# A linear-attention and SwiGLU kernel: PSUM as one rotating pool of single banks, half-height loads in natural head order, stores of 64 partitions, and a reordered start

## The chip, the cores and the metric

The kernel runs on one core of one Trainium2 chip. The time is the device time of one execution in microseconds (us), and I quote the median of several runs. The profile is of one execution; its "span" goes from the first to the last instruction and is about 2 us shorter than the time.

Names of the engines: PE is TensorE (matmuls), PEld its weight loads, DVE is VectorE, ACT is ScalarE, POOL is GpSimd, SP issues transfers. A name with a small q (SPq) is the engine's instruction queue. SBUF and PSUM are the two memories in which the kernel keeps its tiles: tiles of up to 128 partitions in SBUF, which its loads fill, and the tiles in PSUM that its matmuls write.

## The reference

There are 8 batches of 8 heads with 576 positions and head dimension 64; `d_model` is 512, `d_ff` is 1536, and there are 4608 tokens. In float32:

```python
q_s = softmax of q over the head dimension
k_s = softmax of k over the 576 positions
kv  = einsum('bhsd,bhse->bhde', k_s, v)
att = einsum('bhsd,bhde->bhse', q_s, kv)
x   = att.transpose(0, 2, 1, 3).reshape(4608, 512)
out = (silu(x @ w_gate) * (x @ w_val)) @ w_out
```

The two gate and value products and the output product are nearly all of the arithmetic.

## The kernel before

A batch's heads are handled in two groups of four. A group's life is: load q, k, v; exponentials on ACT (`eq`, `ek`) and a cast of v (`vb`); the norm on DVE (`rs`, `rr`, `qs`); nine transposes on PE (`tp`) copied to `qt`; the product `kv`; its scaled block-diagonal copy `bd`; the product `xp`, copied to `xt`. Then come the gate and value matmuls over chunks of tokens (`g_ps`, `u_ps`, the result `hr`) and the output tiles (`o_ps`, copied to `o_sb`, stored). The lines show the parts that changed; cuts are marked.

```python
aps = pool("aps", bufs=1, PSUM)      # one buffer of TWO banks: tp, kv, xp take turns
fps = pool("fps", bufs=6, PSUM)      # six single banks: g_ps, u_ps, o_ps, x_tail
...
def load(b, G, what, src):           # one transfer over all 128 partitions, 576 KB
    t_ = ld.tile([128, 2, T * 64], FP32, tag=what, name=what)
    ap = AP(offset=src[b, 4 * G], ap=[[T * 64, 128], [2 * HSTR, 2], [1, T * 64]])
    dmas[what, b, G] = nc.sync.dma_start(out=t_, in_=ap)
...
def att_exp(b, G):                   # eq and ek on ScalarE, then
    nc.gpsimd.tensor_copy(out=vb[...], in_=raw["v", b, G])
    ...                              # and the norm: rs, rr, qs on VectorE
...
def store(j, o_sb):                  # 128 tokens in one transfer, where both halves are of one batch
    parts = [(0, 128, [[d_model, 2], [T * d_model, 64], [1, d_model]], b0, t0)]
    ...
        nc.sync.dma_start(out=dst, in_=o_sb[p0:p1, :])
...
    for G in range(NG):              # batch 0, before any gate/value matmul
        att_t(0, G); att_kv(0, G); att_x(0, G)
    ...
    for m in range(MT):
        m_unit(0, 576, m)
    o_pair(0); o_pair(2)             # four output tiles, and after them all of batch 1
    for G in range(NG):
        att_exp(1, G)
    for G in range(NG):
        att_t(1, G); att_kv(1, G); att_x(1, G)
    ...
    for ci, (c0, n) in enumerate(chunks):          # (576, 448), then chunks of 512
        ...
        for m in range(MT):                        # 12 units
            if m in (4, 8):
                if att:
                    att_exp(b, ...); steps = att_steps(b, ...)
                if ci > 0:
                    o_pair(...)
            m_unit(c0, n, m)
            if m % 4 > 0 and m > 4 and steps:
                steps.pop(0)()
```

The weights are cut into slices of columns, each loaded by four transfers whose row order fits the head order of the 128-partition loads.

The softmax here doesn't subtract the row's maximum and nothing guards it: scores larger than these inputs give would overflow.

## Time and profile before

The kernel took 381.04 us (median of 3; 379.97 to 381.15). The span of the profiled run is 378.1 us. Four boundaries, all read from the timeline of PE, cut it into stages:

| stage | from | to | us |
|---|---|---|---|
| start and batch 0's gate/value work | 0 | first output tile, 48.93 | 48.9 |
| four output tiles and batch 1's attention | 48.93 | first gate matmul of chunk 576, 77.42 | 28.5 |
| chunk 576..1023 | 77.42 | first gate matmul of the next chunk, 110.75 | 33.3 |
| the other chunks | 110.75 | PE's end, 360.93 | 250.2 |
| tail | 360.93 | 378.1 | 17.2 |

These are lines of the page of the kernel before. The rows of digits show tenths of busy time (or of the granted PE clock) in 40 slices of the span, 9.5 us each. The last line is the chain of waits, by engine.

```profile
span 378.1 us, 4831 instructions
...
PE 320.0 (85%) x1857; PEld 161.1 (43%) x1888; DVE 171.8 (45%) x304; ACT 152.7 (40%) x196; POOL 41.5 (11%) x57
...
PE   0379994487689999999999999999999999999910
...
PEclk9999998578989999999999999999999999999975
DMA  8799951885230606430661246110010011012011
...
PE 77%; DVE 6%; DMA 6%; ACT 4%; issue 2%; SPq 0%; DVEq 0%
```

PE is the bound where its digit is 9. That leaves the first three slices, slices 7 to 12 (57 to 113 us, with the clock low in five of the six), and the last two, in which PE has hardly any work. From slice 13 to there, PE's own work sets the pace. The next view lists the waits of PE (us in total, times, longest).

```profile
PE tp L145 <- DVE qs L132: 19.9, 4, 9.0
PE kv L161 <- DVE qt L149: 9.2, 4, 4.6
PE g_ps L205 <- ACT xt L191: 4.1, 7, 0.6
PE tp L145 <- ACT xt L191: 2.1, 2, 1.0
```

The last line is the price of the single two-bank buffer: the second group's transposes wait until the first group's `xp` is copied away. The timeline shows what happens in the batch 1 stage (start, length, engine, line, operation, and in brackets the idle time before it and its releaser):

```profile
60.58 0.69 DVE L238 COPY o_sb<-o_ps 128x512 f32<-128x512 f32 x1 [2.99 <-DMA out_dram<-o_sb]
...
64.28 1.14 PE L145 MATMUL tp<-ident,qs 128*128 128x128 bf16 x9 [4.83 <-DVE qs L132]
...
68.06 1.16 PE L161 MATMUL kv<-vb_79,ek 64*128 64x129 bf16 x18 [2.63 <-DVE qt L149]
...
72.29 1.12 PE L145 MATMUL tp<-ident,qs 128*128 128x128 bf16 x9 [1.05 <-ACT xt L191]
```

The chain runs through a store: the output copy waits 2.99 us for a buffer that a store still reads, the norm is queued behind that copy on DVE, and PE waits 4.83 us for the norm. Last, three windows of 2 us. The columns are: start and end, length, busy time and count of PE, PEld, DVE, ACT, POOL, then the granted PE clock, the DMA share (mean busy share of the core's 16 DMA engines) and GB/s.

```profile
4.00:6.00 2.00, 0.00 (x0) 0.00 (x0) 0.10 (x1) 1.16 (x1) 0.00 (x0) 1.00 1.05 395
6.00:8.00 2.00, 0.00 (x0) 0.00 (x0) 1.93 (x3) 1.16 (x1) 0.00 (x0) 1.00 1.01 392
92.00:94.00 2.00, 2.00 (x7) 0.76 (x6) 0.94 (x3) 0.39 (x1) 0.00 (x0) 0.50 0.91 308
366.00:368.00 2.00, 0.00 (x0) 0.00 (x0) 0.00 (x0) 0.00 (x0) 0.00 (x0) 0.50 0.13 51
```

At 92 to 94 us the clock is at half. At 366 us only the last stores run, with a share of 0.13 and 51 GB/s: as much as two of 16 engines.

### The profile page before, as it was taken

Reading aid. Unit: us, or ns where it says so; the run is one execution under the profiler, and the core shown is the slowest. Engines: PE = TensorE matmul, PEld = TensorE weight load, DVE = VectorE, ACT = ScalarE, POOL = GpSimd, SP = SyncE. Lnnn points to the kernel's source line nnn. Section 1 sums busy time; section 2 is a strip of 40 time slices with the busy share of each in tenths; the row PEclk is TensorE's granted clock in tenths of the full one; section 3 lists DMA queues with packets and bytes.
Section 4 is the critical chain, followed back from the end, with each engine's and each line's share of the span. In section 5 each row is a group of like instructions: output and inputs, shape, how many; then the busy total and the mean of one; then the engine's idle time right before and its main releaser. Section 6 shows DMA issues by size and latency. Waiting matters only on the chain.

```text
span 378.1 us, 4831 instructions
## 1 busy us (share of the span) xinstructions
PE 320.0 (85%) x1857; PEld 161.1 (43%) x1888; DVE 171.8 (45%) x304; ACT 152.7 (40%) x196; POOL 41.5 (11%) x57
## 2 busy tenths in 40 slices
PE   0379994487689999999999999999999999999910
PEld 0157752333344444444444444444444444444400
DVE  3523436335544664547364727555664333333200
ACT  3333360147736273645466454736273113121000
POOL 2995020011110101010101100110000000000000
PEclk9999998578989999999999999999999999999975
DMA  8799951885230606430661246110010011012011
GB/s 297 135 154 179 289 209 51 284 311 178 83 135 19 211 18 212 142 118 29 217 207 52 56 186 208 40 40 17 31 54 27 10 47 44 13 44 67 18 51 44
DMA packets 24071, 42.78 MB, mean 113 GB/s; under 512 B 1520, under 2 KB 7152, under 8 KB 24048
## 3 DMA queue, kind: packets, MB, share of 16 engines
q1 hardware_dynamic: 17856, 37.75, 28.8%
q0 software_dynamic: 6192, 4.72, 8.9%
q8 instruction: 15, 0.25, 0.3%
q14 instruction: 8, 0.07, 0.1%
HBM read 37.75 MB, written 9.44 MB: 125 GB/s over the span
## 4 chain that ended last, share of the span: by engine, by line
PE 77%; DVE 6%; DMA 6%; ACT 4%; issue 2%; SPq 0%; DVEq 0%
PE u_ps L205 24%; PE g_ps L205 24%; PE o_ps L233 20%; DMA out_dram<-o_sb 4%; PE kv L161 3%; ACT xt L191 3%; PE tp L145 3%; PE xp L183 2%; DMA q<-in_q_dram 2%; DVE qs L132 2%; DVE rs L128 2%; ACT eq L114 1%; DVE qt L149 1%; DVE o_sb L238 1%; ACT L114 1%
## 5 line engine op out<-in xcount | busy, mean ns | idle before, releaser
L213 ACT ACTIVATE sg<-g_ps 128x512 bf16<-128x512 f32 (+2 forms) x120 | 65.0, 554 | 148.9 <-PE g_ps L205 134.6
L214 DVE TENSOR_TENSOR hr<-sg,u_ps 128x512 bf16<-128x512 bf16 (+2 forms) x120 | 74.9, 633 | 108.1 <-PE u_ps L205 106.2
L205 PE MATMUL g_ps<-xt,wg 128*128 128x512 bf16 (+2 forms) x468 | 114.1, 366 | 4.5 <-ACT xt L191 4.1
L205 PE MATMUL u_ps<-xt,wv 128*128 128x512 bf16 (+2 forms) x475 | 112.3, 363 | 0.3
L233 PE MATMUL o_ps<-wo,hr 128*128 128x512 bf16 x422 | 95.3, 379 | 0.5
L205 PEld LDWEIGHTS <-wv 128*128 128x128 bf16 x480 | 47.7, 99 | 48.2 <-issue 2.7
L205 PEld LDWEIGHTS <-wg 128*128 128x128 bf16 x480 | 45.7, 100 | 48.9 <-issue 8.7
L233 PEld LDWEIGHTS <-hr 128*128 128x128 bf16 x432 | 42.0, 98 | 50.2
L238 DVE COPY o_sb<-o_ps 128x512 f32<-128x512 f32 x36 | 23.9, 686 | 32.0 <-PE o_ps L233 26.2
L128 DVE TENSOR_REDUCE rs<-eq 128x18 f32<-128x1152 bf16 x16 | 21.6, 1352 | 33.8 <-ACT eq L114 33.8
L191 ACT CAST xt<-xp 128x1024 bf16<-128x1024 f32 x16 | 16.2, 1012 | 41.8 <-PE x_tail L186 41.8
L145 PE MATMUL tp<-ident,qs 128*128 128x128 bf16 x144 | 12.8, 245 | 22.2 <-DVE qs L132 19.9
L122 POOL CAST vb_79<-v 128x1152 bf16<-128x1152 f32 x8 | 9.8, 1221 | 138.6 <-PE kv L161 90.7
L145 PEld LDWEIGHTS <-qs 128*128 128x128 bf16 x144 | 10.8, 110 | 26.4 <-DVE qs L132 21.2
L132 DVE TENSOR_TENSOR qs<-eq,rr 128x1152 bf16<-128x1152 bf16 x16 | 21.7, 1358 | 0.5
L114 ACT ACTIVATE eq<-q 128x1152 bf16<-128x1152 f32 x16 | 18.6, 1162 | 5.1 <-DMA q<-in_q_dram 5.0
L118 ACT ACTIVATE ek<-k 128x1152 bf16<-128x1152 f32 x16 | 18.4, 1149 | 0.6 <-DMA k<-in_k_dram 0.6
L114 ACT ACT_TABLE_LOAD x14 | 18.0, 1283 | 1.0 <-PEq L322 0.7
L213 ACT ACT_TABLE_LOAD x14 | 18.0, 1283 | 0.2
L122 POOL CAST vb_80<-v 128x1152 bf16<-128x1152 f32 x8 | 9.8, 1223 | 70.2 <-PE kv L161 62.7
L161 PEld LDWEIGHTS <-ek 64*128 64x128 bf16 x288 | 10.2, 107 | 15.8 <-issue 9.1
L149 DVE COPY qt<-tp 128x640 bf16<-128x640 bf16 (+1 forms) x32 | 13.1, 450 | 3.7 <-PE tp L145 3.7
(28 smaller groups left out, 81.5 us busy)
## 6 DMA issues: line engine op xcount, KB each, us to landing
q<-in_q_dram SPq DMA_DIRECT2D x16, 576.0 KB
k<-in_k_dram SPq DMA_DIRECT2D x16, 576.0 KB
v<-in_v_dram SPq DMA_DIRECT2D x16, 576.0 KB
out_dram<-o_sb SPq DMA_DIRECT2D x32, 256.0 KB
wo<-in_moe_w_out_dram POOLq DMA_DIRECT2D x3, 512.0 KB, 9.7
out_dram<-o_sb SPq DMA_DIRECT2D x8, 128.0 KB
wg<-in_moe_w_gate_dram POOLq DMA_DIRECT2D x8, 96.0 KB, 3.3
wv<-in_moe_w_val_dram POOLq DMA_DIRECT2D x8, 96.0 KB, 3.8
```

Of the source, the lines that this page charges most:

```text
L114: nc.scalar.activation(out=eq, in_=raw["q", b, G].rearrange("p h (t d) -> p t h d", d=64), func=AF.Exp)
L122: nc.gpsimd.tensor_copy(out=vb[:, :, 0:128].rearrange("p t (h d) -> p t h d", d=64), in_=raw["v", b, G].rearrange("p h (t d) -> p t h d", ...
L128: nc.vector.reduce_sum(out=rs, in_=eq2, axis=mybir.AxisListType.X)
L132: nc.vector.tensor_mul(qs.rearrange("p t (h d) -> p (t h) d", d=64), eq2, rr.to_broadcast([128, 2 * T, 64]),)
L145: nc.tensor.transpose(out=tp[:, bank, j * 128:(j + 1) * 128], in_=s["qs"][:, t, :], identity=ident)
L161: nc.tensor.matmul(out=kv[:, g, 0:129], lhsT=s["ek"][r, t, :, :].rearrange("p h d -> p (h d)"), rhs=s["vb"][r, t, 0:129], start=(t == 0), ...
L191: nc.scalar.copy(out=xt[:, 2 * G:2 * G + 2, c0:c0 + 512], in_=xp)
L205: nc.tensor.matmul(out=p_[:, 0:w_], lhsT=w[:, kk, ms], rhs=xt[:, kk, c:c + w_], start=(kk == 0), stop=(kk == KT - 1),)
L213: nc.scalar.activation(out=sg[:, 0:w_], in_=g_ps[:, 0:w_], func=AF.Silu)
L214: nc.vector.tensor_mul(hr[:, m, r:r + w_], sg[:, 0:w_], u_ps[:, 0:w_])
L233: nc.tensor.matmul(out=o_ps, lhsT=hr[:, m, r0:r0 + 128], rhs=wo[:, m, :], start=(m == 0), stop=(m == MT - 1),)
L238: nc.vector.tensor_copy(out=o_sb, in_=o_ps)
```

## The change

The intent: every PSUM tile becomes a single bank out of one rotating pool of eight, so that no group waits for another's banks. The q, k and v loads take the heads in their natural order, two transfers of 64 partitions each, so that a weight slice needs one transfer instead of four. A store always has 64 partitions as its first dimension. Batch 0's v is cast on ACT instead of POOL, and its two groups are interleaved. Batch 1's attention is woven between the output tiles. The `xp` eviction is split over two engines, and the last output tile is cut into two halves of columns. The core of the diff, with cuts marked:

```diff
-    aps = pool("aps", bufs=1, PSUM); fps = pool("fps", bufs=6, PSUM)
+    psp = pool("psp", bufs=8, PSUM)
...
     def load(b, G, what, src, second=None, after=None):
-            ap=[[T * 64, 128], [2 * HSTR, 2], [1, T * 64]],
-        dmas[what, b, G] = nc.sync.dma_start(out=t_, in_=ap)
+        for g in range(2):
+            ap = AP(offset=src[b, 4 * G + 2 * g], ap=[[T * 64, 64], [HSTR, 2], [1, T * 64]])
+            d = eng.dma_start(out=t_[64 * g:64 * g + 64], in_=ap)
...
     def w_slice(dst, src, c0, n):
-        for h in range(2):
-            for g in range(2): ...                 # four transfers of 64 rows
+        return nc.gpsimd.dma_start(out=dst[:, :, c0:c0 + n], in_=ap)
...
-        nc.scalar.copy(out=xt[:, 2 * G:2 * G + 2, c0:c0 + 512], in_=xp)
+        nc.scalar.copy(out=xt[:, 2 * G, c0:c0 + 512], in_=xp[0])
+        nc.vector.tensor_copy(out=xt[:, 2 * G + 1, c0:c0 + 512], in_=xp[1])
...
-            parts = [(0, 128, [[d_model, 2], [T * d_model, 64], [1, d_model]], b0, t0)]
+        for half in range(2):
+                ap=[[T * d_model, 64], [1, c1 - c0]],
+            engs[half].dma_start(out=dst, in_=o_sb[64 * half:64 * half + 64, c0:c1])
...
+        att_exp(0, 0, nc.scalar); att_exp(0, 1, nc.scalar)
+        att_norm(0, 0, BANKS); att_t(0, 0, nc.vector); att_kv(0, 0)
+        att_norm(0, 1, BANKS); att_t(0, 1, nc.scalar); att_kv(0, 1)
+        att_bd(0, 0); att_x(0, 0); att_bd(0, 1); att_x(0, 1)
...
-        o_pair(0); o_pair(2)                       # then batch 1's attention
+        att_head(1, 0); o_unit(0); att_head(1, 1)
+        o_unit(1); s0[0](); s0[1](); o_unit(2); s0[2](); s1[0](); s1[1]()
+        o_unit(3); s1[2]()
```

## The prediction

This was written before the changed kernel was built or run.

> **What bounds the kernel now.** TensorE: the page has it busy 320.0 of 378.1 us; the chain of waits is 77% PE. From 110.7 to 360.9 us it is bound for good: PE idles only about 0.64 us per chunk with an attention batch (waits by engine: for the ScalarE copy of xt, 1.01 us). So the gain must come from the ends and the first 110 us. By the timeline and the windows:
> - Start: gate/value matmuls run steadily only from 25.3 us. Both groups of batch 0 go through one PSUM buffer in turn.
> - Batch 1: its output tiles end at 59.5 us, the next chunk starts at 77.4. In between PE has some 6 us of work, and the granted clock falls to 0.50. The chain shows DVE rs and qs behind an o_sb copy that waited 2.99 us for a store, then tp, kv, xp serially.
> - Chunk 576..1023: PE waits 2.4 and 3.6 us for qs, and the clock falls after each.
> - Tail: PE ends at 360.9, the span at 378.1. With only stores running, the windows show DMA share 0.13 and 51 GB/s: 2 of 16 engines. [...] the store's destination starts with a dimension of 2. [...]
>
> **What the change does, in us**
> 1. Stores of 64 partitions[...]. Tail from PE's end: 17.2 now; then half-width copy (est. 0.4), issue 0.5, landing about 2: est. 3.5. Gain 13.5. The o_sb waits go too.
> 2. Start reordered: v cast on ScalarE (1.15), group 1's exp and norm under group 0, no single PSUM buffer. The new limit is v of group 1: it landed by 13.1, and now shares the DMA with weights that start about 1 us earlier; est. 15. Then cast, kv 1.2, bd 1.1, xp 1.2, eviction 0.6: steady at about 20. Gain 5.3. Weights then arrive just in time (est. 2.7 us per slice from 9.3); one DMA for four cuts Pool's issue from 2.4 to about 0.8 per slice.
> 3. Batch 1 woven between output tiles: DVE's order (norm, o_sb, norm, o_sb, qt, bd) makes xp of group 0 wait, about 2.4 us of PE idle. From the end of batch 0's gate/value work to the next chunk: 28.5 now, est. 17.6. Gain 10.9, plus 2.8 at the next chunk's start (no cold clock, no 1.2 us xt wait).
> 4. Chunk 576..1023: head and steps stand at the same units, so both qs waits stay. Gain 0.
> 5. Five later attention chunks: xt eviction split over two engines, 0.64 to about 0.2 each. Gain 2.2.
> 6. Natural head order, doubled loads (0.45 us issue each, off the chain), four small bd multiplies for two: about -0.3.
>
> Sum about 34.5: 381.0 to **346 us**, 8 in 10 between 339 and 354. Chances: faster 0.97, same 0.02, slower 0.01.
>
> **What would show it.** DMA share during stores well above 0.13, a tail under 5 us; steady gate/value work from 19 to 21 us; the chunk at 576 starting near 61 us; two qs waits of 2 to 4 us left in it; 34.8 us per attention chunk.
>
> **What would make it wrong.** Weights or batch 1's v arriving late (gate/value work stalled on DMA between 20 and 44 us); a clock drop in the batch 1 stage (+1.6); the shared pool's rotation making gate/value banks wait for kv or xp releases in every chunk (+5 or more).

13.5 + 5.3 + 10.9 + 2.8 + 0 + 2.2 - 0.3 is 34.4, written there as about 34.5. Before the run it was shown only that the old stores have a share of 0.13; that stores of 64 partitions would have a much larger one was the author's estimate. The runs showed it afterwards: 0.64 in the kernel after, 1.03 in the first store experiment.

The single figures of the steps, in brackets, against the traces of before and after: the half-width copy took 0.42 us (0.4), the issue of a store 0.51 to 0.85 before and 0.47 to 1.05 after (0.5), the last two stores, of 64 KB, landed 1.9 and 2.2 us after their issue (2), and the cast of v on ACT took 1.15 (1.15). In the old start `kv` took 1.16 us (1.2), the wait for `bd` 0.89 (1.1) and `xp` with its tail 1.14 (1.2); the eviction by halves took 0.59 on ACT (0.6). POOL issued the four weight transfers of a slice in 2.37 to 2.58 us before, and one in 0.75 to 0.88 after (2.4 and 0.8). For the 2.7 us per slice: after, the eight slices took 2.9 us each, from the first issue at 11.66 to the last landing at 35.0, with the loads and the transfers of `wo` beside them. The issue of a load took 0.41 to 0.47 us before and 0.60 to 0.61 after (medians; 0.45). "No cold clock" means a granted clock of 0.50 from 66 to 81 us before; after, it was at 1.00 from 66 to 80. The 1.6 us for a clock drop were an estimate; about 1.7 for each fall is what chunk 576 shows below.

## The result, and the profile after

| | median us | runs | ratio to before, 95% interval |
|---|---|---|---|
| before | 380.76 | 4 (379.97 to 381.15) | |
| after | 351.32 | 4 (350.33 to 352.68) | 0.9232 (0.9195 to 0.9268) |

All ratios in this document are the mean time of one kernel's runs over the mean time of the other's runs of the same rounds, so they are not quite the ratio of the quoted medians. Executions over 1.5% slower than the fastest of the same kernel are left out of the means. The kernel became 29.4 us faster, where 34.5 us was predicted. The same boundaries in both timelines say where the gain came from:

| stage | before | after | gain | predicted gain |
|---|---|---|---|---|
| start and batch 0's gate/value work, to | 48.93 | 50.06 | -1.1 | 5.3 |
| output tiles and batch 1, to | 77.42 | 67.98 | 10.6 | 10.9 |
| chunk 576..1023, to | 110.75 | 95.94 | 5.4 | 2.8 (all of it at the chunk's start) |
| other chunks, to | 360.93 | 344.10 | 2.0 | 2.2 |
| tail, to | 378.1 | 348.6 | 12.7 | 13.5 |
| added small costs | | | | -0.3 |
| sum | | | 29.5 | 34.4 |

The lines of the page after that answer to those shown of before:

```profile
span 348.6 us, 5035 instructions
...
PE 317.0 (91%) x1900; PEld 159.5 (46%) x1900; DVE 188.5 (54%) x354; ACT 152.6 (44%) x217; POOL 27.2 (8%) x31
...
PE   0269998998699999999999999999999999999994
...
PEclk9999999899999999999999999999999999999999
DMA  7999998999602990299029902990202021102123
```

The slices here are 8.7 us. The hole in slices 7 to 12 is mostly closed (what is left of it, digits of 8, 8 and 6, holds the waits shown below), the idle slices at the end are gone, and the clock dips in one slice. By the chain of waits PE's share rose from 77% to 80%. The first three slices are no better. The DMA row is fuller (slices of 9 where there were 4 and 6), though the bytes are the same (42.81 MB, and 42.78 before); that is the first sign of the miss. The waits of PE after:

```profile
PE tp L152 <- DVE qs L138: 19.4, 4, 9.9
PE xp L192 <- DVE bd_78 L184: 2.0, 2, 1.6
...
PE g_ps L213 <- DVE xt L201: 0.9, 5, 0.2
```

The waits of `kv` for `qt` (9.2 us) and of `tp` for `xt` (2.1 us) have left the list, and the steady wait for `xt` went from 4.1 us to 0.9. New, and left out here, are two waits of `kv` for `vb` at the start (1.6 and 1.3 us). The waits for `bd` are about as large as before (3.6 us over both groups then and now). Windows of the kernel after:

```profile
4.00:6.00 2.00, 0.00 (x0) 0.00 (x0) 0.00 (x0) 0.00 (x0) 0.00 (x0) 1.00 1.06 222
6.00:8.00 2.00, 0.00 (x0) 0.00 (x0) 0.70 (x1) 1.16 (x1) 0.00 (x0) 1.00 1.04 219
92.00:94.00 2.00, 2.00 (x27) 1.09 (x25) 1.44 (x4) 0.54 (x1) 0.00 (x0) 1.00 0.12 27
344.00:346.00 2.00, 0.11 (x1) 0.00 (x0) 0.42 (x1) 0.00 (x0) 0.00 (x0) 1.00 0.64 158
```

Here is the miss. In the same windows, with only the same loads running, the rate is 219 to 222 GB/s instead of 392 to 395, while the share is still about 1.05: all 16 engines are busy, and together they get just over half as much done (219 over 392 is 0.56). That is another picture than the old tail, where the share itself was 0.13. The third line has the clock at 1.00 where it was 0.50, which will matter below. The last line shows the new stores at a share of 0.64. The timeline shows the consequences at the start, and what stayed in the middle:

```profile
11.66 0.88 POOL L94 DMA_DIRECT2D wg<-in_moe_w_gate_dram  x1 [10.36 <-DMA v<-in_v_dram]
...
19.15 1.15 ACT L106 CAST vb_77<-v 128x1152 bf16<-128x1152 f32 x1 [1.38 <-DMA v<-in_v_dram]
...
61.06 0.39 PE L192 MATMUL xp<-qt,bd_78 128*128 128x512 bf16 x1 [1.57 <-DVE bd_78 L184]
...
80.12 0.68 PE L152 MATMUL tp<-ident,qs 128*128 128x128 bf16 x9 [2.41 <-DVE qs L138]
...
91.18 0.68 PE L152 MATMUL tp<-ident,qs 128*128 128x128 bf16 x9 [3.10 <-DVE qs L138]
```

The lines of the kernel before that answer to the cast of `vb_77` and to the two waits for `qs`:

```profile
13.10 1.75 POOL L122 CAST vb_80<-v 128x1152 bf16<-128x1152 f32 x1 [0.69 <-DMA v<-in_v_dram]
...
91.14 0.95 PE L145 MATMUL tp<-ident,qs 128*128 128x128 bf16 x9 [2.41 <-DVE qs L132]
...
104.37 0.68 PE L145 MATMUL tp<-ident,qs 128*128 128x128 bf16 x9 [3.61 <-DVE qs L132]
```

The second group's v reaches its cast at 19.15 us; in the kernel before, with its loads at 392 to 407 GB/s, the same cast started at 13.10. The first weight transfer starts only at 11.66, so weights cannot be what slows the loads at 4 to 8 us. In the middle the wait of `xp` for `bd` and the two waits for `qs` are there, as predicted. After the first of them the clock was at 0.50 from 62 to 64 us; after the two for `qs` it stayed at 1.00.

### The profile page after: what moved, and what is told of

It reads as the page before. It is cut to its first block, busy times and chain, and to the rows that moved or that the text cites. A ratio compares the mean times of both kernels' runs of the same rounds, so it can differ in the third digit from the quotient of the medians.

```text
span 348.6 us, 5035 instructions
## 1 busy us (share of the span) xinstructions
PE 317.0 (91%) x1900; PEld 159.5 (46%) x1900; DVE 188.5 (54%) x354; ACT 152.6 (44%) x217; POOL 27.2 (8%) x31
## 2 busy tenths in 40 slices
DMA packets 25577, 42.81 MB, mean 123 GB/s; under 512 B 2896, under 2 KB 8784, under 8 KB 25552
## 4 chain that ended last, share of the span: by engine, by line
PE 80%; DVE 7%; DMA 7%; ACT 3%; issue 1%; SPq 1%; DVEq 0%; ACTq 0%
PE u_ps L213 25%; PE g_ps L213 25%; PE o_ps L238 24%; DMA v<-in_v_dram 5%; PE kv L168 2%; PE tp L152 2%; DMA k<-in_k_dram 2%; DVE xt L201 1%; DVE hr L222 1%; PE xp L192 1%; DVE qs L138 1%; DVE rs L132 1%; ACT L118 1%; ACT eq L118 1%; SPq L76 1%
## 5 line engine op out<-in xcount | busy, mean ns | idle before, releaser
L238 PE MATMUL o_ps<-wo,hr 128*128 128x512 bf16 x420 | 94.1, 380 | 0.0
L238 PEld LDWEIGHTS <-hr 128*128 128x128 bf16 x420 | 40.7, 98 | 49.0 <-issue 0.8
L243 DVE COPY o_sb<-o_ps 128x512 f32<-128x512 f32 x35 | 23.2, 685 | 22.1 <-PE o_ps L238 22.1
L152 PE MATMUL tp<-ident,qs 128*128 128x128 bf16 x144 | 12.2, 236 | 19.5 <-DVE qs L138 19.4
L138 DVE TENSOR_TENSOR qs<-eq,rr 128x1152 bf16<-128x1152 bf16 (+2 forms) x18 | 21.9, 1224 | 0.5
L108 POOL CAST vb_76<-v 128x1152 bf16<-128x1152 f32 x7 | 9.2, 1310 | 150.3 <-DMA v<-in_v_dram 89.1
L152 PEld LDWEIGHTS <-qs 128*128 128x128 bf16 x144 | 9.9, 105 | 24.0 <-DVE qs L138 21.2
L200 ACT CAST xt<-xp 128x512 bf16<-128x512 f32 x16 | 9.4, 586 | 17.6 <-PE xp L192 9.4
L201 DVE CAST xt<-xp 128x512 bf16<-128x512 f32 x16 | 10.9, 684 | 3.4 <-PE x_tail L195 3.4
L108 POOL CAST vb_77<-v 128x1152 bf16<-128x1152 f32 x7 | 9.0, 1289 | 44.9 <-DMA v<-in_v_dram 24.9
## 6 DMA issues: line engine op xcount, KB each, us to landing
wv<-in_moe_w_val_dram POOLq DMA_DIRECT2D x2, 384.0 KB, 12.2
```

Of the source, the lines that this page charges most:

```text
L108: eng.tensor_copy(out=out, in_=in_)
L138: nc.vector.tensor_mul(qs[:, t0:t1, :].rearrange("p t (h d) -> p (t h) d", d=64), eq2[:, 2 * t0:2 * t1, :], rr[:, 2 * t0:2 * t1].to_broadc ...
L152: nc.tensor.transpose(out=tp[:, j * 128:(j + 1) * 128], in_=s["qs"][:, t, :], identity=ident)
L201: nc.vector.tensor_copy(out=xt[:, 2 * G + 1, c0:c0 + 512], in_=xp[1])
L238: nc.tensor.matmul(out=o_ps, lhsT=hr[:, m, r0:r0 + 128], rhs=wo[:, m, :], start=(m == 0), stop=(m == MT - 1),)
L243: nc.vector.tensor_copy(out=o_sb, in_=o_ps)
```

## The experiments

Twelve kernels ran, and all gave correct results. The diffs below are shortened, and words in them stand for code that is left out. The questions were: why the start gained nothing; how much each of the stores and the PSUM pool is worth; and whether the waits that the timeline names really cost what they show.

### The start: why are the loads slow?

The theory: it is the 64 destination partitions. The rivals: the number and size of the loads, their order in memory, or the weight transfers. The first experiment gives the kernel after the 128-partition loads of the kernel before, with the head order and the four transfers per weight slice that belong to them.

```diff
 def load(...):                      # in the kernel after
-    for g in range(2):
-        ap=[[T * 64, 64], [HSTR, 2], [1, T * 64]]; d = eng.dma_start(out=t_[64*g:64*g+64], in_=ap)
+    ap=[[T * 64, 128], [2 * HSTR, 2], [1, T * 64]]; d = nc.sync.dma_start(out=t_, in_=ap)
 def w_slice(...):
-    one transfer
+    four transfers of 64 rows, as before the change
```

> The changed kernel with the head order of before: each q, k, v tensor of a group is one load over all 128 partitions, and each weight slice four casting loads, as before. Theory A (a load that writes only partitions 0-63 or 64-127 moves about 228 GB/s, half of the 408 GB/s of a 128-partition load): the loads run at about 400 GB/s again, v of group 1 lands at about 14 to 15 us instead of 19.1, gate/value matmuls run steadily from about 20.5 instead of 26.5 us, and the total falls by about 6 us to 345. Theory B (weights and loads contend, or the chain of batch 0 is what it is): no change, 350 to 352 us.

In the two traces the rates are 219 to 230 GB/s from 4 to 14 us in the kernel after, and 392 to 407 from 4 to 10 us in the kernel before (408 from 4 to 5).

Measured: 347.16 us (343.84 to 349.79), ratio 0.910 (0.9033 to 0.9166). One of the four runs, 349.79, counts as slow and is not in the ratio; the median of the three fast ones is 345.41. The spread goes with the clock: the two runs with a mean clock of 0.995 took 345.41 and 343.84, mean 344.6. The two runs of the kernel after with that clock took 350.33 and 350.88, mean 350.6. At equal clock the difference is therefore 6.0 us. The profiled run fits theory A; windows of this experiment:

```profile
4.00:6.00 2.00, 0.00 (x0) 0.00 (x0) 0.35 (x1) 1.16 (x1) 0.00 (x0) 1.00 1.09 348
90.00:92.00 2.00, 2.00 (x18) 0.95 (x18) 0.47 (x1) 0.51 (x1) 0.00 (x0) 0.50 0.00 0
```

The loads are back at 348 GB/s (337 in the next window). They are not at 392, and three of the first slice's four weight transfers are issued from 1.28 us on and run beside them, because only the last carries the wait for v; whether that is the reason was not tested. The cast of the second v starts at 14.00 instead of 19.15, gate work at 20.07 instead of 25.29, and the output tiles at 45.31 instead of 50.06. The second line is a warning: in this run the clock fell after both waits for `qs`, and chunk 576 took 31.4 us where the kernel after, with the same order, took 28.0.

The second experiment keeps the halves but puts one half of each of batch 0's loads on ACT's queue, so that both halves of the partitions are filled at the same time.

```diff
-    load(b, G, what, src, nc.scalar if (b, G, what) == (0, 0, "q") else None, after)
+    load(b, G, what, src, nc.scalar if b == 0 else None, after)
```

> The changed kernel, natural head order kept; the second 64-partition half of every load of batch 0 is issued from the Activation queue, so that the two halves are in flight together. Theory A [...]: both halves together reach about 400 GB/s, v of group 1 lands at 14 to 15 us, total about 345 to 346 us. Rival C (64-partition, 288 KB loads are slow in themselves, by size or by number): the rate stays near 228 GB/s, total 351 us.

Measured: 349.27 us (347.54 to 349.92), ratio 0.9177 (0.9143 to 0.9211). A miss: 2 us, not 6. The windows show that the rate did not come back:

```profile
4.00:6.00 2.00, 0.00 (x0) 0.00 (x0) 0.00 (x0) 0.00 (x0) 0.00 (x0) 1.00 1.06 247
6.00:8.00 2.00, 0.00 (x0) 0.00 (x0) 0.00 (x0) 0.18 (x1) 0.00 (x0) 1.00 1.04 221
```

From 2 to 10 us the four windows have 207, 247, 221 and 263 GB/s, mean 234; the kernel after has 205, 222, 219 and 230, mean 219. That is 7% more, not twice as much. From 10 to 14 us, with weight transfers to all 128 partitions beside the loads, two windows have 333 and 339 GB/s where the kernel after has 224 and 230, and the cast of the second v starts at 16.27, 2.9 us earlier than in that kernel; why the rate rises then was not followed. Besides, ACT was busy issuing transfers until 7.8 us, and its first exponential started at 9.23. My expectation took the halves for independent. With only loads running they were not: 234 GB/s with both halves on their way, 219 with one after the other.

The third experiment is the one that separates the rivals. It also makes two loads of 288 KB per tensor with the same bytes and the same rows as the kernel after has, but each load goes to all 128 partitions and to half of the free dimension.

```diff
-        for g in range(2):
-            offset=src[b, 4 * G + 2 * g], ap=[[T * 64, 64], [HSTR, 2], [1, T * 64]]
-            d = eng.dma_start(out=t_[64 * g:64 * g + 64], in_=ap)
+        for h in range(2):
+            offset=src[b, 4 * G + 2 * h], ap=[[T * 64, 128], [1, T * 64]]
+            d = eng.dma_start(out=t_[:, h, :], in_=ap)
```

> As the run with 128-partition loads, but each load is cut into two of 288 KB by its second dimension: all 128 partitions, one head each, the same descriptor size, number and size of DMAs as in the changed kernel. Theory A (partitions count): 400 GB/s, as the 128-partition run, about 345 us. Rival C (twice as many, half as large loads are the cost): 228 GB/s and about 351 us.

Measured: 347.66 us (345.78 to 350.11), ratio 0.9146 (0.9093 to 0.9199). A window of this experiment:

```profile
4.00:6.00 2.00, 0.00 (x0) 0.00 (x0) 0.00 (x0) 1.10 (x1) 0.00 (x0) 1.00 1.08 310
```

The cast of the second v started at 14.18 us. So neither the number nor the size nor the source of the loads is the main cause; the spread over the partitions is. At 310 (308 in the next window) the rate is below the 348 of the first experiment, so the number and size may explain that smaller part. The weight transfers differ as well in both experiments; the fourth shows that they are not the cause of the low rate. Loads to 64 partitions had 222 GB/s where loads to 128 had 395, which is 0.56 of it. Why the partitions should do this, no run here shows.

The fourth experiment puts the half-height loads, with the single weight transfer per slice, into the kernel before. I held it to be harmless there.

```diff
 def load(...):                      # in the kernel before
-    ap=[[T * 64, 128], [2 * HSTR, 2], [1, T * 64]]; one transfer
+    two transfers: t_[64*g:64*g+64] <- ap=[[T * 64, 64], [HSTR, 2], [1, T * 64]]
 def w_slice(...):
-    four transfers of 64 rows
+    one transfer of 128 rows
```

> The kernel before with only the natural head order: 64-partition loads on one queue and one casting load per weight slice. Theory A: its loads fall to about 228 GB/s, v of group 1 lands at 18 to 19 us instead of 13.1, but there kv of group 1 waits until 21.1 us for the single PSUM buffer anyway, so the total moves by at most 1 us: 380 to 382 us. The slower loads are free in the old order and cost 6 us in the new one. If instead the total rises by 5 us or more, the loads were on the critical path before too.

Measured: 384.09 us (383.8 to 384.64), ratio 1.0105 (1.0073 to 1.0136). A miss: it costs 4.0 us, which is clear of the noise. Two windows of this run:

```profile
4.00:6.00 2.00, 0.00 (x0) 0.00 (x0) 0.00 (x0) 0.06 (x1) 0.00 (x0) 1.00 1.07 242
6.00:8.00 2.00, 0.00 (x0) 0.00 (x0) 0.00 (x0) 1.99 (x2) 0.00 (x0) 1.00 1.06 240
```

The kernel before has 395 and 392 there. No weight transfer has been issued in either kernel by then (the first comes at 12.42 here and at 9.90 there), so the shape of the loads alone takes the rate away. The timeline of this run:

```profile
18.61 1.16 PE L159 MATMUL kv<-vb,ek 64*128 64x129 bf16 x18 [5.94 <-DVE qt L147]
```

In the kernel before this matmul starts at 14.73, after a wait of 4.58. On DVE, `qt` of the first group stands behind the norm of the second group, which needs the second group's q. So the later load delays the first group too: 3.9 us at `kv`, and 3.8 us at the first output tile (52.69 against 48.93).

### The stores

The kernel before gets the new stores and nothing else; the kernel after gets the old ones.

```diff
 def store(j, o_sb):                 # the kernel before, first experiment
-    parts = [(0, 128, [[d_model, 2], [T * d_model, 64], [1, d_model]], b0, t0)]
+    for half in range(2): ap=[[T * d_model, 64], [1, d_model]]
 def store(j, o_sb, c0, c1, engs):   # the kernel after, second experiment
-    for half in range(2): ap=[[T * d_model, 64], [1, c1 - c0]]
+    parts = [(0, 128, [[d_model, 2], [T * d_model, 64], [1, n]], b0, t0)]
```

> The kernel before with only the stores of the change: two stores of 64 partitions per output tile instead of one of 128 with a leading dimension of 2. Theory: the DMA share during a store rises well above 0.13, the tail from PE's end to the end of the span falls from 17.2 to about 4 us, and the o_sb copy of batch 1's stage no longer waits 2.9 us (worth about 1 us of chain): 381 to about 366 to 367 us. If the tail is set by something else (a fixed cost at the end), less than 5 us.

> The changed kernel with only the stores of before. Theory: the tail is back at about 16 to 17 us instead of 4.7, plus 1 to 3 us where stores on 2 engines make o_sb copies or the loads behind them in the queue wait in batch 1's stage: 351 to about 363 to 366 us. If it is under 358, the stores' gain overlaps with what the rest of the change gives.

Measured: the kernel before with new stores took 366.27 us (363.27 to 367.48), ratio 0.9617 (0.9565 to 0.9669); beside it before took 380.37, so the gain is 14.1. The kernel after with old stores took 365.86 us (364.73 to 367.11), ratio 0.9619, which is 14.5 more than the 351.32 of the kernel after (measured in another set of runs, against the same kernel before). The two agree, partly by luck: of the 15.5 us that the profiled run of the second lost, 13.8 lie in the tail and 3.4 in chunk 576, where its clock fell twice, while the batch 1 stage was 1.5 us faster. The tails of the profiled runs, from PE's end to the end of the span, are 5.0 us (361.4 - 356.43) with the new stores and 18.3 us (364.1 - 345.77) with the old. Windows of each tail, first two (one of 2 and one of 0.5 us) of the kernel before with the new stores, then one of the kernel after with the old:

```profile
358.00:360.00 2.00, 0.00 (x0) 0.00 (x0) 0.00 (x0) 0.00 (x0) 0.00 (x0) 0.77 0.60 131
359.00:359.50 0.50, 0.00 (x0) 0.00 (x0) 0.00 (x0) 0.00 (x0) 0.00 (x0) 0.59 1.03 221
```

```profile
350.00:352.00 2.00, 0.00 (x0) 0.00 (x0) 0.00 (x0) 0.00 (x0) 0.00 (x0) 0.50 0.13 51
```

The share of 0.13 comes back with the leading dimension of 2, though the last tile is still cut into two column halves, and so still stored by two transfers. So the shape of the stores makes the tail, and the cut of the last tile does not. In all four kernels the share goes with the leading dimension: 0.13, as much as 2 of 16 engines, where it is 2, and with the new stores, where it is 64, 0.64 in the kernel after and up to 1.03 in the window of 0.5 us. No other leading dimension was tried. The rate in that window is 221 GB/s: here stores from 64 partitions kept all engines busy (share 1.03) and still went no faster than the loads to 64 partitions (219 to 230).

### The PSUM pool

The first attempt gave the kernel after the old pools back, with `tp`, `kv` and `xp` as halves of one two-bank buffer. With one buffer the first group has to finish before the second starts, so its order changed as well.

```diff
-    psp = pool("psp", bufs=8, PSUM)
+    aps = pool("aps", bufs=1, PSUM); fps = pool("fps", bufs=6, PSUM)
 def att_t(b, G, eng):
-    for t0, t1 in BANKS:
-        tp = psp.tile([128, 1024], BF16)
+    tp2 = aps.tile([128, 2, 1024], BF16)
+    for bank, (t0, t1) in enumerate(BANKS):
+        tp = tp2[:, bank, :]
...                                   # kv and xp likewise; att_t(0, 1) after att_x(0, 0)
```

> The changed kernel with the PSUM layout of before (one buffer of two banks for tp, kv and xp in turn, six single banks for the rest); the order of batch 0 has to be serial per group for it, since the woven order would wait for itself. Theory: the shared pool of 8 is what allows the weaving, so the serial waits come back: 2 to 5 us in the first two stages, little in the steady chunks (up to 0.3 us each): 354 to 357 us. If the pool does nothing by itself, 351 to 352.

Measured: 381.11 us (380.63 to 383.28), ratio 1.003 (0.9989 to 1.0071). A miss by about 25 us, and the edit itself is to blame. A line of its timeline:

```profile
65.41 0.59 PE L157 MATMUL tp<-ident,qs 128*128 128x128 bf16 x4 [4.09 <-DVE qt L112]
```

The second half of the transposes now waits (4.09 us in this line) for the copy of the first half, because both are in one tile and the loop copies in between. The list of waits has 16.9 us of this, in 15 waits. The kernel before does not do that: it does all nine transposes and then both copies. The second attempt does the same.

```diff
     for bank, (t0, t1) in enumerate(BANKS):
         ...transposes of this bank...
+    for bank, (t0, t1) in enumerate(BANKS):
         copy(eng, qt[:, :, t0:t1, :], ...)
```

> The run with the old PSUM layout gave 381 us, 30 more than the changed kernel and far from the 354 to 357 expected. Its trace shows a wait that the edit brought in: the copy out of the first bank of tp stands between the transposes of the two banks, and since both are one tile the second part waits for the copy of the first (16.9 us in 15 waits, 4.1 us in batch 1's stage). Here all nine transposes come first, as in the kernel before. Theory: 10 to 17 us of the 30 go away, 362 to 371 us, and what is left over 351 is what two-bank tiles in one buffer cost by themselves: serial groups in the first two stages, and the two evictions of xp, which on one tile run one after the other. If it stays above 376, the transposes' waits were harmless and the single buffer is the whole cost.

Measured: 367.36 us (366.68 to 368.64), ratio 0.9653 (0.9628 to 0.9677). Within what was expected: about 16 us slower than the kernel after. By the stage boundaries of the profiled runs, 4.3 us are lost before the first output tile (54.31), 6.3 in the batch 1 stage (24.2 against 17.9), 4.4 in chunk 576 (32.4 against 28.0) and 3.3 in the rest (251.4 against 248.2). Its timeline and its waits:

```profile
21.65 0.69 DVE L210 CAST xt<-xp 128x512 bf16<-128x512 f32 x1 [1.80 <-ACT xt L209]
```

```profile
PE xp L201 <- DVE bd L192: 7.8, 2, 6.1
```

The copy of `xp` on DVE now waits for the copy on ACT (1.80 us idle; it starts at 21.65, and the copy on ACT ran from 21.03 to 21.61), since both read one tile; the split over two engines gained nothing here, where the tile was not split as well. The 16 us are the value of the pool together with the interleaving that it allows; the two were not separated, and part of the loss in chunk 576 is the clock (mean 0.981).

### The order of the middle, and a faster version

The kernel after still had waits for `bd` and for `qs` in the middle. The next kernel starts from the one with 128-partition loads, moves the copies of the batch 1 stage to ACT, does both norms before the output tiles and both `bd` before `xp`, and starts the attention of chunk 576 at units 2 and 6. Batch 0 gets the same treatment (both `bd` before `xp`, one copy of `xt` moved to ACT), which the expectation does not mention: gate work starts at 18.13 us, against 20.07 in the first experiment.

```diff
-        att_head(1, 0); o_unit(0); att_head(1, 1); ...
+        att_head(1, 0); att_head(1, 1); load_batch(2)
+        o_unit(0, nc.scalar); o_unit(1, nc.scalar)
+        att_t(1, 0, nc.scalar); att_kv(1, 0); att_bd(1, 0)
+        o_unit(2, nc.scalar)
+        att_t(1, 1, nc.scalar); att_kv(1, 1); att_bd(1, 1); att_x(1, 0)
+        o_unit(3); att_x(1, 1)
...
+            heads = (2, 6) if ci == 0 else (4, 8)
```

> A version meant to beat both: the changed kernel with 128-partition loads (first experiment), batch 1's copies out of PSUM moved to ScalarE and both norms put ahead of bd on DVE, so that xp of group 0 does not wait (2.0 us of PE idle and the clock drop after it), and in the chunk at 576 the heads issued at units 2 and 6 instead of 4 and 8, so that the qs latency of 5.6 us lies under four gate/value units instead of two (qs waits 2.4 and 3.1 us). Expected: about 345 less 3 and less 5: 336 to 340 us, granted clock 0.995 or more in most runs. If the waits only move to the gate/value banks or to the loads, 343 to 346.

Measured: 343.88 us (342.93 to 344.5), ratio 0.9032 (0.8997 to 0.9067). A miss. At the start of chunk 576 this kernel was 11.6 us ahead of the kernel after (56.37 against 67.98), at its end only 5.2 (90.70 against 95.94). The timeline shows where the lead went:

```profile
60.09 0.69 DVE L111 COPY o_sb<-o_ps 128x512 f32<-128x512 f32 x1 [4.87 <-DMA out_dram<-o_sb]
...
61.43 0.53 PE L216 MATMUL g_ps<-xt,wg 128*128 128x448 bf16 x1 [4.15 <-DVE xt L111]
```

The fourth output copy waits 4.87 us on DVE for a store that stands behind batch 2's loads; the `xt` copy is queued behind it, and PE waits for that. Later PE waits 3.06 us for `bd`, which stands behind the second head's norm on DVE. Both are orders that I had made. The next kernel gives `o_sb` six buffers and starts the heads at units 1 and 6.

```diff
+    osp = pool("osp", bufs=6)
-        o_sb = ff.tile([128, 512], FP32)          # 3 buffers
+        o_sb = osp.tile([128, 512], FP32)
-            heads = (2, 6) if ci == 0 else (4, 8)
+            heads = (1, 6) if ci == 0 else (4, 8)
+            pops = (4, 5, 7, 9, 10, 11) if ci == 0 else (5, 6, 7, 9, 10, 11)
```

> The reordered version missed (343.9 for 336 to 340): its trace shows the batch 1 stage done 12 us earlier than in the changed kernel, then 4.15 us of PE waiting for a DVE xt copy behind an o_sb copy that waited 4.87 us for a store, which sat behind batch 2's loads; and 3.06 us of xp waiting for bd behind the next group's norm; the clock fell after both. Here o_sb has six buffers instead of three, and in the chunk at 576 the heads stand at units 1 and 6 with kv and bd of group 0 before the second head. Expected: both waits gone, 333 to 337 us, granted clock about 0.99. If the stores' delay only moves on to another wait: 340 or more.

Measured: 333.44 us (332.74 to 334.55, 5 runs), ratio 0.8763 (0.8742 to 0.8784). It beats both kernels. From its page and its waits:

```profile
span 331.0 us, 4939 instructions
...
PEclk9999999999999999999999999999999999999999
```

```profile
PE tp L156 <- DVE qs L142: 11.5, 2, 8.3
PE g_ps L217 <- DVE xt L112: 1.0, 5, 0.2
```

The two waits for `qs` in chunk 576 are gone (2 waits left of 4, both at the start), and in this run the clock never falls. What the six buffers alone are worth was not measured. Two more kernels take one thing back each. The first puts the heads back to units 4 and 8:

```diff
-            heads = (1, 6) if ci == 0 else (4, 8)
-            pops = (4, 5, 7, 9, 10, 11) if ci == 0 else (5, 6, 7, 9, 10, 11)
+            heads = (4, 8)
+            pops = (5, 6, 7, 9, 10, 11)
```

> As the second reordered version, with the heads of the chunk at 576 back at units 4 and 8. Theory: the two qs waits of 2.4 and 3.1 us come back, with or without a clock drop after each (1.5 us): 5 to 8 us slower than the second reordered version, 340 to 344 us. If it is within 2 us of it, those waits were not on the critical path.

Measured: 339.86, 340.45 and 340.1 us, ratio 0.8934 (0.8913 to 0.8955). So the place of the heads is worth about 6.7 us (340.1, the middle one of the three, less 333.44). In the kernel after the two waits are 2.41 and 3.10 us, 5.5 together. The clock does not explain the rest, since the run of 340.45 us had a mean clock of 1.0. Where it goes I could not see, since the profile fell on the fourth run, which took 674.12 us and is left out. Its mean recorded clock was 1.0, yet the output matmuls took 680 ns on average, against 380 in the kernel after, while the evictions on DVE (690 and 685) and the activations on ACT (554 in both) were as fast as ever. The second gives that kernel the half-height loads of the kernel after:

```diff
-        ap=[[T * 64, 128], [2 * HSTR, 2], [1, T * 64]]; d = nc.sync.dma_start(out=t_, in_=ap)
+        for g in range(2):
+            ap=[[T * 64, 64], [HSTR, 2], [1, T * 64]]; d = eng.dma_start(out=t_[64*g:64*g+64], in_=ap)
 def w_slice(...):
-    four transfers of 64 rows
+    one transfer
```

> The second reordered version (333.4 us) with the change's own loads and weight slices back: natural head order, 64-partition loads. The first comparison of load rates (351.3 against 347.2) was blurred by a clock that fell in some runs and not in others; the second reordered version holds a granted clock of 1.0, so the cost of the loads should stand clear. Theory A: loads at about 228 GB/s again, v of group 1 lands at about 19 us instead of 13.5 to 14, gate/value matmuls start 5 to 6 us later, nothing makes it up: 339 to 342 us. If batch 1's or 2's loads then also come late, 343 to 347. If the loads' rate does not matter: 333 to 335.

Measured: 341.49 us (340.08 to 341.66, 5 runs), ratio 0.8964 (0.894 to 0.8987). That is 8.05 us more than the kernel with 128-partition loads; both ran at a mean clock of about 1.0, so the clock has no part in it (they ran on different chips, and the ratios, 2.0% apart, say 7.6 us). In the profiled runs gate work starts at 23.98 us instead of 18.19 (5.8), the first output tile at 48.89 instead of 41.89 (7.0), and chunk 576 at 64.51 instead of 55.96 (8.6; in the batch 1 stage PE now waits 1.46 us for the cast of v); after that the two are alike (248.3 and 248.1 us from the next chunk to PE's end).

## Why the prediction was right or wrong

The direction, and the range of 339 to 354 us, held. The gain was 29.4 us where 34.5 was predicted. That it came so near is partly luck: the start missed by 6.4 us, and 2.6 of it came back in chunk 576, mainly because the clock did not fall there in the profiled run. Step by step:

1. **Stores.** Right. Predicted 13.5 us from the tail, measured 12.7 (17.2 to 4.5); the share rose from 0.13 to 0.64. The two store experiments show that the shape of the stores is the cause. They give 14.1 and 14.5 us in all; of the first, 12.2 lie in the tail (17.17 to 4.97), and the rest, which is less than the spread of its runs (363.27 to 367.48), was not followed.
2. **Start.** Wrong, and this is the step that failed. The prediction wrote of the second group's v that it "landed by 13.1, and now shares the DMA with weights that start about 1 us earlier; est. 15", and in step 6 it booked "doubled loads (0.45 us issue each, off the chain)". It counted the loads and not the partitions they go to. The runs showed 219 to 230 GB/s instead of 392 to 407 before any weight was issued, the v cast at 19.15 us, and gate work from 25.29 us (at full pace, counted back from the first output tile at 1.96 us per unit, from about 26.5) instead of "about 20". The estimated gain of 5.3 us became a loss of 1.1. With 128-partition loads the output tiles start 4.75 us earlier (45.31 against 50.06), which is most of the missing 6.4; there gate work starts at 20.07, as predicted, but the clock then fell to 0.50 (22 to 24 us), and this work took 25.2 us instead of the 23.6 of full pace, which is the other 1.7. The experiment that splits the loads by the free dimension excludes their number, size and source as the main cause. "The chunk at 576 starting near 61 us" failed for the same reason: it was 68.0, and with 128-partition loads 63.3.
3. **Batch 1 woven in.** Right: predicted 10.9, measured 10.6 (28.5 to 17.9 us). The wait of `xp` for `bd` is there, 1.57 us in the line shown and 2.0 with the matmul after it, against the 2.4 predicted, and the clock dropped after it, which the prediction had named as a danger (+1.6) and not put into the sum. So the near hit is partly luck: in the experiment with the old stores, in the same order, the clock did not drop in this stage, and it took 16.4 us. With the old pools the stage takes 24.2 us.
4. **Chunk 576.** The waits were right and the sizes were off. Both waits for `qs` stayed, 2.41 and 3.10 us, as predicted. But the chunk gained 5.4 us where 2.8 was put down for its start and nothing for the rest. By the two timelines its start (up to the third gate unit) gained only 1.6 us (5.1 to 3.5; PE's idle time for `xt` in it was 0.30 us before, where the prediction has 1.2), the shorter second wait gave 0.5, and the clock that did not fall after the two waits gave 1.7 and 1.6. The last part is luck: in the same order the chunk took 28.0 us with no fall in it (the kernel after), 29.7 with one (the second and the third experiment) and 31.4 with two (128-partition loads, and old stores), about 1.7 us for each. Why waits of about the same length sometimes cost the clock (2.41 us before, to 0.50) and sometimes not (2.41 us after, at 1.00) was not shown; no run here varied this alone. Runs of the kernel after at mean clocks of 0.995 and 0.988 are about 1.6 us apart (350.6 and 352.2).
5. **Later chunks.** Right: predicted 2.2, measured 2.0; a chunk with attention takes 35.0 us where 35.3 was measured before and 34.8 predicted. The wait for `xt` per chunk fell from 0.64 to about 0.2 us, and it is still there in the best version.
6. **Sum of small costs.** The -0.3 us cannot be seen on its own. The costly part of "natural head order, doubled loads" was in step 2.

The danger that the prediction named last, "the shared pool's rotation making gate/value banks wait", did not appear: `g_ps` waits for `xt` alone, 0.9 us in all. The change thus gave away about 6 us, most of it at its own start, by taking half-height loads for the sake of a simpler weight transfer. What the four weight transfers alone cost or save was not measured apart from the loads.

## What to carry to other kernels

Before changing the shape of a transfer, look at both its DMA share and its GB/s: here a low share meant that few engines worked (a leading dimension of 2: share 0.13, 51 GB/s), and a full share at a low rate went with where the data went (64 partitions: share 1.05, about 222 instead of 395 GB/s; it cost 4.0, 6.0 and 8.05 us in three kernels, each with the weight transfers that go with the loads). When work is woven between other work, follow every in-order queue and every buffer that it passes through: the same idea lost its lead to one copy that waited 4.87 us for a store, and with more buffers and earlier heads it gave 333.4 us. Remove the gaps of 2 to 3 us in PE's work first: in chunk 576 some of them also cost the clock, about 1.7 us for each fall.
